# Attention followed by a max-of-products layer: half-walked conversion pieces, and GpSimd's weight and x pieces in other steps

## The chip, the cores and the metric

The kernel runs on one core of one Trainium2 chip. The metric is the device time of one execution in microseconds.

## The reference

```python
scores = np.matmul(q, k.transpose(0, 1, 3, 2)) / np.sqrt(D) + bias   # bias: a small MLP on the relative position
attn = softmax(scores)                                               # with 1e-9 added to the sum
x = np.matmul(attn, v)                                               # (4, 8, 576, 64), then (2304, 512)
h = np.maximum(np.maximum(x @ w1, x @ w2), x @ w3)                   # w: 512 x 768
out = h @ w_out                                                      # 768 x 512
```

q, k and v are (4, 8, 576, 64), B = 4 batches and H = 8 heads. The weights of the second half lie in memory as 8-byte floats; the output is float32, 2304 x 512.

## The kernel before

The work comes in three stages. First the bias tables are made (until about 48 us). Then attention runs, 72 steps in eight rounds of nine; n is the step, n % 9 its position. Last comes the layer behind attention, here called moe, three products whose maximum is taken and an output product, written as schemes of seven block products.

**A step of attention.** Every engine runs its instructions in the order in which the program gives them, so the code's order is the schedule. Step n issues: the scores of step n on PE (front, L287; one step in nine is made of remainders, L277); for each of two heads a shift on DVE (L297: bias added, minimum found) into a tile sn of which three exist; the exponential on ACT (L311) and, every second step, a small copy of the sums (L314, tile sm). The step before last gets its sums' reciprocal on DVE (L321, rc, every second step) and is normalised on GpSimd (norm, L325, two instructions, e<-e,rc). The step four back is turned on PE (flip, L352), copied out by ACT (L458) and DVE (L462, tile et), and later multiplied by v on PE (L393). At two or four positions of a round the q and k of a coming pair are split into a high and a low part, by a cast on ACT (L243, tiles kh and qh) and a subtraction on GpSimd (L249, tiles kl and ql). L285 to L287 use the parts in three matmuls.

**Conversion.** The weights lie in memory as 8-byte floats. fetch (L577) loads half a block as pairs of 32-bit words, and convert (L580) makes float32 from them in five instructions: L584 on ACT (scaled magnitude of the high words, tile wa), and four pieces on DVE: L586 (maximum with 2), L588 (shift and mask), L591 (the low words shifted and joined in) and L594 (the sign joined in, result wr). L586 and L588 have one source, wa, and write it in place; L591 and L594 have two. convert is a generator: it yields "scalar" or "vector" ahead of each piece. A Stream (L517) holds such a generator and takes one piece forward when its next word is the wanted one. A step calls the streams in its list once with "vector" (between, in the midst of the step, behind the et copies and ahead of rc) and once with "scalar" (at its end).

first (L1142) converts six halves during attention, of the sets named 2, 0 and 1. Making the Stream runs it to its first yield. GpSimd's own work on the weights waits in a list, pend: sums of blocks (sums, tile ws, four pieces) and low parts (tile wl, four pieces). In conv, up to two entries of pend are taken out each time that a conversion piece is due, and stand on GpSimd then. early_x makes the parts of the first x block from step 36 on: b12l, b11l and t1l on GpSimd (L535), their casts on ACT, the sum t1 on DVE. The list of streams of a step is made at the end of the program:

```python
if n >= NS - 2 and n % NS in (0, 2, 4, 6, 7):
    more += [w0]
if n >= 36 and n % NS in (2, 6, 7):
    more.insert(0, ex)
```

w0 is the Stream of first, ex that of early_x. Of first only the head, conv and the two blank pieces matter here:

```python
ahead = [fetch(wpool, *todo.pop(0))]
pend = []
def conv(out, name):
    if todo:
        ahead.append(fetch(wpool, *todo.pop(0)))
    for token in convert(wpool, ahead.pop(0), out, name):
        yield token
        if token == "vector":
            for f in pend[:2]:
                pend.pop(0)()
for _ in range(2):
    yield "vector"
```

In moe the same convert makes 18 more halves beside the products, in slots of its own.

Of the kernel before, what the change touches and what calls it, by code (L numbers as in the profile page):

```python
# [9 lines left out]
F32 = mybir.dt.float32  # L10
F32R = mybir.dt.float32r
U32 = mybir.dt.uint32
ACTF = mybir.ActivationFunctionType
ALU = mybir.AluOpType
# [5 lines left out]
def kernel(  # L20
# [12 lines left out]
    nc = tc.nc  # L33
# [165 lines left out]
    NS = len(STEPS)  # L199
# [12 lines left out]
    class Attention:  # L212
        def __init__(self, pool):
            self.pool = pool
            self.data = {}
            self.st = {}
            self.et = {}
            self.pvq = []
            self.done = []
            self.sums = []  # L220
            bias_t.extend(pool.tile([128, 2, S], F32, name=f"bias{t}", bufs=1) for t in range(NTQ + 1))
            self.vl = [pool.tile([128, 2, D], F32, name=f"vl{x}", bufs=1) for x in range(2)]
            for x in self.vl:
                nc.gpsimd.memset(x, 0.0)
# [292 lines left out]
    class Stream:  # L517
# [6 lines left out]
        def go(self, scalar):  # L524
            if self.next == ("scalar" if scalar else "vector"):
                self.next = next(self.gen, None)
                return True

        def rest(self):
            while self.next:  # L530
                self.next = next(self.gen, None)

    def arith(eng, out, a, b, op=ALU.subtract):
        f = lambda x: x.bitcast(F32) if x.dtype == F32R else x
        eng.tensor_tensor(out=out, in0=f(a), in1=f(b), op=op)  # L535
# [37 lines left out]
    def fetch(pool, srcs, name):  # L573
        w = pool.tile([128, 512, 2], U32, tag="w64", bufs=2, name=f"w64{name}")
        n = 512 // len(srcs)
        for x, src in enumerate(srcs):
            nc.sync.dma_start(out=w[:, n * x:n * x + n].rearrange("p (c f) t -> p c (f t)", c=src.shape[1]), in_=src)  # L577
        return w

    def convert(pool, w, out, name):  # L580
        a = pool.tile([128, 512], F32, tag="wa", bufs=1, name=f"wa{name}")
        high, low, t = w[:, :, 1], w[:, :, 0], a.bitcast(U32)
        yield "scalar"
        nc.scalar.activation(a, high.bitcast(F32), ACTF.Abs, scale=2.0 ** 16)  # L584
        yield "vector"
        nc.vector.tensor_scalar(out=a, in0=a, scalar1=2.0, scalar2=None, op0=ALU.max)  # L586
        yield "vector"
        nc.vector.tensor_scalar(out=t, in0=t, scalar1=3, scalar2=0x7FFFFFFF,  # L588
                                op0=ALU.logical_shift_left, op1=ALU.bitwise_and)
        yield "vector"  # L590
        nc.vector.scalar_tensor_tensor(out=t, in0=low, scalar=29, in1=t,  # L591
                                       op0=ALU.logical_shift_right, op1=ALU.bitwise_or)
        yield "vector"
        nc.vector.scalar_tensor_tensor(out=out() if callable(out) else out, in0=high, scalar=signm,  # L594
                                       in1=t, op0=ALU.bitwise_and, op1=ALU.bitwise_or)
# [5 lines left out]
    def w_srcs(s, d):  # L601
        fp, i = divmod(s, 3)
        m = (mw1, mw2, mw3)[i]
        return [m[256 * d:256 * d + 256, 256 * (2 * fp + b):256 * (2 * fp + b) + 256].rearrange(
            "(c p) f -> p c f", p=128) for b in range(2)]
# [4 lines left out]
    def raw_tile(pool, s):  # L610
        return pool.tile([128, 1024], F32, tag=f"wr{s % 2}", bufs=1, name=f"wr{s}")

    def sum_tile(wpool, s):
        return wpool.tile([128, 1024], F32, tag="ws", bufs=1, name=f"ws{s}")

    def part(t, n):
        return t[:, 256 * n:256 * n + 256]

    def sum_w(raw, sr):
        g = nc.gpsimd  # L620
        for o, a, b, op in ((part(sr, 0), part(raw, 0), part(raw, 2), ALU.add),
                            (part(sr, 1), part(sr, 0), part(raw, 1), ALU.subtract),
                            (part(sr, 2), part(raw, 1), part(raw, 0), ALU.subtract),
                            (part(sr, 3), part(raw, 3), part(sr, 1), ALU.subtract)):
            yield "vector"
            arith(g, o, a, b, op)
# [468 lines left out]
    with tc.manual_schedule():  # L1095
        nc.vector.memset(signm, 0x80000000)
        psums.append(tc.alloc_tile_pool(name="psum_b", bufs=1, space=PSUM))
        apool = tc.alloc_tile_pool(name="attn_p", bufs=1, side="right")
        at = Attention(apool)
        n = 0  # L1100
# [36 lines left out]

        last = {}

        def first():  # L1140
            todo = [(w_srcs(s, d), f"{s}_{d}") for s in (PARK, 0, 1) for d in range(2)]
            ahead = [fetch(wpool, *todo.pop(0))]  # L1142

            pend = []

            def conv(out, name):
                if todo:
                    ahead.append(fetch(wpool, *todo.pop(0)))
                for token in convert(wpool, ahead.pop(0), out, name):
                    yield token  # L1150
                    if token == "vector":
                        for f in pend[:2]:
                            pend.pop(0)()

            def sums(raw, name, k=None):
                got = {}

                def piece(n):
                    if n == 0:
                        got["sr"] = sum_tile(wpool, name)  # L1160
                        got["gen"] = sum_w(raw, got["sr"])
                        next(got["gen"])
                    next(got["gen"], None)
                    if n == 3 and k is not None:
                        nc.sync.dma_start(out=w_d[k, 1], in_=got["sr"])
                    return got["sr"]

                return [lambda n=n: piece(n) for n in range(4)]

            def block(name):  # L1170
                made = []

                def half(d):
                    if d == 0:
                        made.append(raw_tile(wpool, 1))
                    return made[0][:, 512 * d:512 * d + 512].bitcast(U32)

                return made, half

            for _ in range(2):  # L1180
                yield "vector"
            made, half = block("2")
            for d in range(2):
                yield from conv(lambda: half(d), f"2_{d}")
            nc.sync.dma_start(out=w_d[0, 0], in_=made[0])
            pend.extend(sums(made[0], "2", 0))
            hi, lo = (wpool.tile([128, 1792], F32R, tag=f"w{c}0", bufs=1, name=f"w{c}0") for c in "hl")
            wf[0] = (hi, lo)
            made, half = block("0")
            for d in range(2):  # L1190
                r = slice(512 * d, 512 * d + 512)
                yield from conv(lambda: half(d), f"0_{d}")
                raw = made[0]
                yield "scalar"
                nc.scalar.copy(hi[:, r], raw[:, r])
                pend.extend(lambda k=k, raw=raw: arith(nc.gpsimd, part(lo, k), part(raw, k), part(hi, k))
                            for k in range(2 * d, 2 * d + 2))
            made, half = block("1")
            for d in range(2):
                yield from conv(lambda: half(d), f"1_{d}")  # L1200
            for f in sums(made[0], "1"):
                yield "vector"
                sr = f()
            last.update(raw=made[0], sr=sr)

        w0 = Stream(first())
        x0 = Blocks(0, xa, xa)

        def early_x():
            g = nc.gpsimd  # L1210
            for k in ("b12", "b11"):
                yield "scalar"
                x0.high(k)
                yield "vector"
                x0.low(k, g)
            yield "vector"
            x0.sum("t1")
            yield "scalar"
            x0.high("t1")
            yield "vector"  # L1220
            x0.low("t1", g)

        def late_x():
            for k in ("b21", "b22"):
                yield "scalar"
                x0.high(k)
                yield "vector"
                x0.low(k, nc.gpsimd)

        ex, lx = Stream(early_x()), Stream(late_x())  # L1230
        while n < NSTEP + LAG:
            more = []
            if n >= NS - 2 and n % NS in (0, 2, 4, 6, 7):
                more += [w0]
            if n >= 36 and n % NS in (2, 6, 7):
                more.insert(0, ex)
            if n >= NSTEP:
                more.insert(0, lx)
            at.step(n, more)
            n += 1  # L1240
        while at.pvq:
            at.pvq.pop(0)()
        for w in (w0, ex, lx):
            w.rest()
        x0.sum("t3")
        x0.high("t3")
# [55 lines left out]
```

## Time and profile before

| what | us |
|---|---|
| runs, median of three | 543.1 |
| runs, lowest and highest | 538.97, 543.71 |
| the profiled execution's own time | 542.02 |
| its span, first to last instruction | 540.2 |

The profiled execution is one execution more, taken by the hardware profiler, and all rows come from it. Its span leaves out 1.8 us around the instructions. In rows, PE is the matrix engine, PEld its weight load, DVE the vector engine, ACT the scalar engine, POOL is GpSimd and SP the queue that issues DMAs. A name such as wa<-w is a destination and its source; x18 counts instructions. Idle time in brackets stands before an instruction, with what ended it. The granted clock is a share of full speed.

### The profile page before, as it was taken

Reading aid. Unit: us, or ns where it says so; the run is one execution under the profiler, and the core shown is the slowest. Engines: PE = TensorE matmul, PEld = TensorE weight load, DVE = VectorE, ACT = ScalarE, POOL = GpSimd, SP = SyncE. Lnnn points to the kernel's source line nnn. Section 1 sums busy time; section 2 is a strip of 40 time slices with the busy share of each in tenths; the row PEclk is TensorE's granted clock in tenths of the full one; section 3 lists DMA queues with packets and bytes.
Section 4 is the critical chain, followed back from the end, with each engine's and each line's share of the span. In section 5 each row is a group of like instructions: output and inputs, shape, how many; then the busy total and the mean of one; then the engine's idle time right before and its main releaser. Section 6 shows DMA issues by size and latency. Waiting matters only on the chain.

```text
span 540.2 us, 13662 instructions
## 1 busy us (share of the span) xinstructions
PE 527.9 (98%) x5199; PEld 439.3 (81%) x5199; DVE 436.9 (81%) x915; ACT 360.0 (67%) x810; POOL 266.8 (49%) x294
## 2 busy tenths in 40 slices
PE   8999899999999899999999999999999999999997
PEld 5455667666767566667599999999999999999997
DVE  7997879899888998878598988658887447898883
ACT  7998889898999898988677433443334325455552
POOL 0003777779878887875500665646466435400000
PEclk9999989999999999999999999999999999999999
DMA  5895976635755165211301125441266340756642
GB/s 164 243 333 174 348 236 197 206 93 158 225 168 150 24 194 160 69 23 23 119 1 41 40 78 183 149 157 42 77 243 204 127 157 0 240 170 196 186 147 79
DMA packets 73458, 78.66 MB, mean 146 GB/s; under 512 B 23152, under 2 KB 54512, under 8 KB 73392
## 3 DMA queue, kind: packets, MB, share of 16 engines
q1 hardware_dynamic: 73248, 77.49, 46.1%
q8 instruction: 41, 0.67, 0.5%
q10 hardware_dynamic: 144, 0.29, 0.2%
q14 instruction: 25, 0.20, 0.1%
HBM read 49.56 MB, written 27.94 MB: 143 GB/s over the span
## 4 chain that ended last, share of the span: by engine, by line
PE 84%; DVE 8%; issue 3%; POOL 2%; ACT 2%; DMA 1%; DVEq 0%; POOLq 0%; ACTq 0%
PE pv L393 13%; PE p L645 11%; PE p L643 11%; PE p L644 11%; PE s L287 10%; PE tp L352 5%; PE p_o L1021 4%; PE p_o L1020 4%; PE p_o L1019 4%; DVE hid L113 4%; PE bp L135 3%; DVE sn L297 2%; PE c L643 2%; PE c L645 2%; PE c L644 2%
## 5 line engine op out<-in xcount | busy, mean ns | idle before, releaser
L325 POOL TENSOR_SCALAR e<-e,rc 128x576 f32<-128x576 f32 x144 | 110.2, 782 | 40.1 <-DVE rc L321 35.0
L297 DVE CUSTOM_DVE_ANT_0 sn<-s,bias 128x576 f32<-128x576 f32 x144 | 103.1, 753 | 26.1 <-PE lp L352 11.8
L311 ACT ACTIVATE e<-sn,nm 128x576 f32<-128x576 f32 x144 | 111.4, 780 | 8.7 <-DVE nm L297 7.4
L393 PE MATMUL pv<-et,vt 128*64 128x320 f32 (+1 forms) x496 | 74.7, 422 | 0.1
L462 DVE COPY et<-tp 128x512 f32<-128x512 f32 x72 | 49.3, 685 | 7.8 <-PE tp L352 6.1
L535 POOL TENSOR_TENSOR wl<-wr,wh 128x256 fp32r<-128x256 f32 x25 | 24.6, 1011 | 58.6 <-ACT wh L731 58.6
L352 PE MATMUL tp<-ident,e 64*128 64x64 f32 x1152 | 52.9, 224 | 0.0
L287 PE MATMUL s<-kh,qh 64*128 64x288 f32 x240 | 49.4, 343 | 3.3 <-DVE nm L297 3.1
L458 ACT COPY et<-tp 128x512 f32<-128x512 f32 x72 | 41.8, 581 | 13.5 <-PE lp L352 11.0
L287 PEld LDWEIGHTS s<-kh,qh 64*128 64x128 f32 x240 | 28.8, 186 | 24.4 <-DVE nm L297 12.3
L352 PEld LDWEIGHTS tp<-ident,e 64*128 64x128 f32 x1152 | 47.2, 139 | 0.0
L393 PEld LDWEIGHTS pv<-et,vt 128*64 128x64 f32 x496 | 30.5, 137 | 18.3 <-issue 2.1
L287 PE MATMUL s<-kl,qh 64*128 64x288 f32 x240 | 42.0, 299 | 0.0
L135 PE MATMUL bp<-hid,w2s 128*32 128x79 f32 (+51 forms) x640 | 39.9, 390 | 0.9 <-DVE hid L113 0.7
L287 PE MATMUL s<-kh,ql 64*128 64x288 f32 x240 | 40.6, 294 | 0.0
L113 DVE TENSOR_SCALAR hid<-sm,bp 128x528 f32<-128x528 f32 (+17 forms) x108 | 39.1, 438 | 0.0
L535 POOL TENSOR_TENSOR wl<-ws,wh 128x256 fp32r<-128x256 f32 x28 | 30.7, 1128 | 12.9 <-ACT wh L733 12.9
L135 PEld LDWEIGHTS bp<-hid,w2s 128*32 128x32 f32 x640 | 19.9, 109 | 21.1 <-issue 15.5
L352 PE MATMUL lp<-ident,e 64*128 64x64 f32 x144 | 33.3, 231 | 3.3 <-ACT et L458 2.4
L690 ACT COPY u<-p 128x384 f32<-128x384 f32 x24 | 11.5, 480 | 37.2 <-PE p L645 37.2
L535 DVE TENSOR_TENSOR q<-p,u 128x384 f32<-128x384 f32 x36 | 19.9, 553 | 17.2 <-ACT u L690 14.2
L352 PEld LDWEIGHTS lp<-ident,e 64*128 64x128 f32 x144 | 19.8, 137 | 16.5 <-POOL e L325 8.5
(232 smaller groups left out, 1617.8 us busy)
## 6 DMA issues: line engine op xcount, KB each, us to landing
bias_d<-bs SPq DMA_DIRECT2D x36, 295.5 KB, 5.2
bias<-bias_d SPq DMA_DIRECT2D x16, 576.0 KB, 5.3
w<-in_moe_w_dram SPq DMA_DIRECT2D x36, 256.0 KB, 3.3
h_d<-ht SPq DMA_DIRECT2D x18, 384.0 KB, 3.3
hin<-h_d SPq DMA_DIRECT2D x16, 384.0 KB, 4.5
qr<-in_qd_dram SPq DMA_DIRECT2D x16, 288.0 KB, 4.7
kr<-in_kd_dram SPq DMA_DIRECT2D x16, 288.0 KB, 4.8
vt<-in_v_dram SPq DMA_DIRECT2D x32, 128.0 KB, 3.2
```

What stands on the lines that cost most here:

```text
L113: marks["hid"] = nc.vector.tensor_scalar(out=h[:, 0:n], in0=wl[:, 0:n], scalar1=k["bp"][:, m:m + 1], scalar2=0.0, op0=ALU.add, op1=ALU.max)
L135: nc.tensor.matmul(bp[32 * c:32 * c + 32, o:o + w], lhsT=w2s, rhs=src, start=True, stop=True)
L287: nc.tensor.matmul(ss[h][:, x, 0:HALF], lhsT=u[q][p, 128 * t:128 * t + 128], rhs=u[k][p, cols], start=(j == 0), stop=(j == len(terms) - 1))
L297: nc.vector.tensor_tensor_reduce(out=sn.rearrange("p (a b) -> p a b", a=2), in0=st["s"][h][:, :, 0:HALF], in1=bt.rearrange("p (a b) -> p a ...
L311: nc.scalar.activation(st["e"][:, S * h:S * h + S], sn, ACTF.Exp, scale=-1.0, bias=nm, accum_out=self.sm[:, x:x + 1])
L325: nc.gpsimd.tensor_scalar(out=e, in0=e, scalar1=self.rc[:, x:x + 1], scalar2=1.0, op0=ALU.mult, op1=ALU.mult)
L352: return nc.tensor.transpose(to, e2[p, k0:k0 + 128], ident[p, p])
L393: nc.tensor.matmul(pv[p], lhsT=w, rhs=x, start=(c == 0), stop=(c == NTQ))
L535: eng.tensor_tensor(out=out, in0=f(a), in1=f(b), op=op)
L643: nc.tensor.matmul(o, lhsT=hi[:, c], rhs=h[:, j], start=first and j == 0, stop=False, **on)
L644: nc.tensor.matmul(o, lhsT=hi[:, c], rhs=l[:, j], start=False, stop=False, **on)
L645: nc.tensor.matmul(o, lhsT=lo[:, c], rhs=h[:, j], start=False, stop=last and j == 1, **on)
```

## The change

Four edits. The two one-source pieces of convert walk wa as 128 x 2 x 256, first the even and then the odd elements, still in place. The list pend becomes an object Pieces with a place of its own in the steps: one entry at positions 1, 3, 5 and 8, while conversion keeps positions 0, 4, 6 and 7, and x pieces get 3 and 8. The block of set 2 gets a buffer of its own, wr2, and set 1 takes out what is left of pend before it takes a buffer. And the two blank "vector" pieces at the head of first go, so that the generator's first yield is that of the first conversion.

```diff
--- before.py
+++ after.py
@@ -583,9 +583,11 @@
         yield "scalar"
         nc.scalar.activation(a, high.bitcast(F32), ACTF.Abs, scale=2.0 ** 16)
         yield "vector"
-        nc.vector.tensor_scalar(out=a, in0=a, scalar1=2.0, scalar2=None, op0=ALU.max)
+        apart = a.rearrange("p (n k) -> p k n", k=2)
+        nc.vector.tensor_scalar(out=apart, in0=apart, scalar1=2.0, scalar2=None, op0=ALU.max)
         yield "vector"
-        nc.vector.tensor_scalar(out=t, in0=t, scalar1=3, scalar2=0x7FFFFFFF,
+        apart = apart.bitcast(U32)
+        nc.vector.tensor_scalar(out=apart, in0=apart, scalar1=3, scalar2=0x7FFFFFFF,
                                 op0=ALU.logical_shift_left, op1=ALU.bitwise_and)
         yield "vector"
         nc.vector.scalar_tensor_tensor(out=t, in0=low, scalar=29, in1=t,
@@ -1137,20 +1139,34 @@
 
         last = {}
 
+        class Pieces:
+
+
+            def __init__(self):
+                self.todo = []
+
+            def extend(self, fs):
+                self.todo.extend(fs)
+
+            def go(self, scalar):
+                if self.todo and not scalar:
+                    self.todo.pop(0)()
+
+            def rest(self):
+                while self.todo:
+                    self.todo.pop(0)()
+
+        pend = Pieces()
+
         def first():
             todo = [(w_srcs(s, d), f"{s}_{d}") for s in (PARK, 0, 1) for d in range(2)]
             ahead = [fetch(wpool, *todo.pop(0))]
-
-            pend = []
 
             def conv(out, name):
                 if todo:
                     ahead.append(fetch(wpool, *todo.pop(0)))
                 for token in convert(wpool, ahead.pop(0), out, name):
                     yield token
-                    if token == "vector":
-                        for f in pend[:2]:
-                            pend.pop(0)()
 
             def sums(raw, name, k=None):
                 got = {}
@@ -1171,14 +1187,16 @@
                 made = []
 
                 def half(d):
-                    if d == 0:
+                    if d == 0 and name == "2":
+                        made.append(apool.tile([128, 1024], F32, name="wr2", bufs=1))
+                    elif d == 0:
+                        if name == "1":
+                            pend.rest()
                         made.append(raw_tile(wpool, 1))
                     return made[0][:, 512 * d:512 * d + 512].bitcast(U32)
 
                 return made, half
 
-            for _ in range(2):
-                yield "vector"
             made, half = block("2")
             for d in range(2):
                 yield from conv(lambda: half(d), f"2_{d}")
@@ -1230,9 +1248,11 @@
         ex, lx = Stream(early_x()), Stream(late_x())
         while n < NSTEP + LAG:
             more = []
-            if n >= NS - 2 and n % NS in (0, 2, 4, 6, 7):
+            if n >= NS - 2 and n % NS in (0, 4, 6, 7):
                 more += [w0]
-            if n >= 36 and n % NS in (2, 6, 7):
+            if n % NS in (1, 3, 5, 8):
+                more += [pend]
+            if n >= 36 and n % NS in (3, 8):
                 more.insert(0, ex)
             if n >= NSTEP:
                 more.insert(0, lx)
@@ -1240,7 +1260,7 @@
             n += 1
         while at.pvq:
             at.pvq.pop(0)()
-        for w in (w0, ex, lx):
+        for w in (w0, pend, ex, lx):
             w.rest()
         x0.sum("t3")
         x0.high("t3")
```

On ACT, steps 6 to 10, before: wa is the conversion's tile, e and sm belong to the softmax, et to the turned products, kh to the split of k.

```order
L314 ACTIVATE sm_1120<-sm_1120 128x4
L311 ACTIVATE e_1268,sm_1269<-sn_0_1265,nm_0_1266 128x576
L311 ACTIVATE e_1268,sm_1269<-sn_1_1271,nm_1_1272 128x576
L458 COPY et_1_1218<-tp_5_0_1280 128x8x64
L458 COPY et_1_1218<-lp_5_1279 128x128
L311 ACTIVATE e_1325,sm_1269<-sn_0_1322,nm_0_1323 128x576
L458 COPY et_1_1130<-tp_3_0_1333 128x8x64
L458 COPY et_1_1130<-lp_3_1332 128x128
L311 ACTIVATE e_1325,sm_1269<-sn_1_1327,nm_1_1328 128x576
L314 ACTIVATE sm_1269<-sm_1269 128x4
L243 CAST kh_1363<-kr_1051 128x576
L584 ACTIVATE wa_0_1362<-w_0_1181 128x512
```

And with the change, in the same place:

```order
L314 ACTIVATE sm_1120<-sm_1120 128x4
L584 ACTIVATE wa_0_1187<-w_0_1181 128x512
L311 ACTIVATE e_1273,sm_1274<-sn_0_1270,nm_0_1271 128x576
L311 ACTIVATE e_1273,sm_1274<-sn_1_1276,nm_1_1277 128x576
L458 COPY et_1_1222<-tp_5_0_1285 128x8x64
L458 COPY et_1_1222<-lp_5_1284 128x128
L311 ACTIVATE e_1330,sm_1274<-sn_0_1327,nm_0_1328 128x576
L458 COPY et_1_1130<-tp_3_0_1338 128x8x64
L458 COPY et_1_1130<-lp_3_1337 128x128
L311 ACTIVATE e_1330,sm_1274<-sn_1_1332,nm_1_1333 128x576
L314 ACTIVATE sm_1274<-sm_1274 128x4
L243 CAST kh_1365<-kr_1051 128x576
```

L584 stood behind four exponentials, two pairs of et copies and a kh cast; now it stands behind the sm copy of step 7 and ahead of all of them.

On POOL around step 45, before (b12l and b11l are parts of x, wl of a weight, kl and ql of k and q):

```order
L535 TENSOR_TENSOR b12l_3471<-xb_0_1169,b12h_3220 128x768
L325 TENSOR_SCALAR e_3338<-e_3338,rc_3473 128x576 x2
L535 TENSOR_TENSOR b11l_3537<-xb_0_1170,b11h_3477 128x768
L325 TENSOR_SCALAR e_3409<-e_3409,rc_3473 128x576 x2
L325 TENSOR_SCALAR e_3467<-e_3467,rc_3595 128x576 x2
L535 TENSOR_TENSOR wl_2319<-wr_2766,wh_2318 128x256 x2
L325 TENSOR_SCALAR e_3533<-e_3533,rc_3595 128x576 x2
L249 TENSOR_TENSOR kl_3666<-kr_3356,kh_3665 128x576
```

And with the change:

```order
L325 TENSOR_SCALAR e_3335<-e_3335,rc_3464 128x576 x2
L325 TENSOR_SCALAR e_3401<-e_3401,rc_3464 128x576 x2
L535 TENSOR_TENSOR b12l_3582<-xb_0_1169,b12h_3281 128x768
L325 TENSOR_SCALAR e_3459<-e_3459,rc_3584 128x576 x2
L325 TENSOR_SCALAR e_3522<-e_3522,rc_3584 128x576 x2
L249 TENSOR_TENSOR kl_3655<-kr_3348,kh_3654 128x576
L535 TENSOR_TENSOR wl_2381<-wr_2954,wh_2380 128x256
L325 TENSOR_SCALAR e_3574<-e_3574,rc_3717 128x576 x2
L249 TENSOR_TENSOR ql_3722<-qr_3349,qh_3721 128x576
L325 TENSOR_SCALAR e_3647<-e_3647,rc_3717 128x576 x2
L535 TENSOR_TENSOR b11l_3845<-xb_0_1170,b11h_3588 128x768
L535 TENSOR_TENSOR wl_2381<-wr_2954,wh_2380 128x256
```

The two wl ahead of a product of L325 and a kl are gone; one wl stands behind kl, and another comes behind b11l, later.

On SP, from the last bias table to the next loads of q and k, before:

```order
L170 DMA bias_d<-bs_878 16x8x591
L577 DMA w_0_1181<-in_moe_w_dram 128x2x256 x2
L259 DMA vt_1184<-in_v_dram 128x4x64
L260 DMA vl_80<-in_v_dram 64x64
L259 DMA vt_1184<-in_v_dram 128x4x64
L260 DMA vl_80<-in_v_dram 64x64
L230 DMA qr_1305<-in_qd_dram 128x576
L231 DMA kr_1304<-in_kd_dram 128x576
L577 DMA w_1_1359<-in_moe_w_dram 128x2x256 x2
```

And with the change:

```order
L170 DMA bias_d<-bs_878 16x8x591
L577 DMA w_0_1181<-in_moe_w_dram 128x2x256 x2
L577 DMA w_1_1184<-in_moe_w_dram 128x2x256 x2
L259 DMA vt_1188<-in_v_dram 128x4x64
L260 DMA vl_80<-in_v_dram 64x64
L259 DMA vt_1188<-in_v_dram 128x4x64
L260 DMA vl_80<-in_v_dram 64x64
L230 DMA qr_1310<-in_qd_dram 128x576
L231 DMA kr_1309<-in_kd_dram 128x576
```

The second fetch moved from behind six loads to a place directly behind the first fetch.

## Rows read from the trace of the kernel before

**Rows 1.** The page, part 1: engine, busy us (share of the span), instructions.

```profile
PE 527.9 (98%) x5199; PEld 439.3 (81%) x5199; DVE 436.9 (81%) x915; ACT 360.0 (67%) x810; POOL 266.8 (49%) x294
```

**Rows 2.** The chain that ended last, from 80 to 340 us: start, us, what.

```profile
108.80 1.13 PE s L277 x16
...
135.08 1.13 PE s L277 x16
...
189.76 1.27 PE s L277 x16
...
216.86 1.13 PE s L277 x16
...
243.04 1.15 PE s L277 x16
```

**Rows 3.** Timeline of DVE at two places: start us, us, line, operation, out<-in.

```profile
177.89 4.31 DVE L586 TENSOR_SCALAR wa<-wa 128x512 f32<-128x512 f32 x1
182.12 0.74 DVE L297 CUSTOM_DVE_ANT_0 sn<-s,bias 128x576 f32<-128x576 f32 x1
...
198.75 1.74 DVE L594 SCALAR_TENSOR_TENSOR wr<-w,signm,wa 128x512 uint32<-128x512 uint32 x1
```

**Rows 4.** Timeline of POOL at the same two places.

```profile
177.64 1.45 POOL L535 TENSOR_TENSOR wl<-wr,wh 128x256 fp32r<-128x256 f32 x2
179.05 1.50 POOL L325 TENSOR_SCALAR e<-e,rc 128x576 f32<-128x576 f32 x2
180.48 1.44 POOL L249 TENSOR_TENSOR kl<-kr,kh 128x576 fp32r<-128x576 f32 x1
...
198.09 1.84 POOL L535 TENSOR_TENSOR t1l<-t,t1h 128x768 fp32r<-128x768 f32 x1
```

**Rows 5.** Timeline of PE there, the waits in brackets (idle before, releaser).

```profile
182.93 0.40 PE L287 MATMUL s<-kh,qh 64*128 64x288 f32 x1 [1.28 <-DVE nm L297]
...
201.21 0.40 PE L287 MATMUL s<-kh,qh 64*128 64x288 f32 x1 [0.21 <-DVE nm L297]
```

**Rows 6.** Instructions on the tile wa, whole span: duration ns min/median/max, first, last start.

```profile
L586 DVE TENSOR_SCALAR wa<-wa x18: 409/866/4307, 78.6 to 407.4; 128x512 f32<-128x512 f32 x18
...
L591 DVE SCALAR_TENSOR_TENSOR wa<-w,wa x18: 681/693/1231, 90.5 to 410.5; 128x512 uint32<-128x512 uint32 x18
L594 DVE SCALAR_TENSOR_TENSOR wr<-w,signm,wa x18: 744/756/1739, 94.1 to 411.2; 128x512 uint32<-128x512 uint32 x18
```

**Rows 7.** Timeline of ACT from 66.9 to 74.7 us, idle time before in brackets.

```profile
66.94 0.20 ACT L314 ACTIVATE sm<-sm 128x4 f32<-128x4 f32 x1
67.27 0.78 ACT L311 ACTIVATE e<-sn,nm 128x576 f32<-128x576 f32 x1
...
70.16 0.78 ACT L311 ACTIVATE e<-sn,nm 128x576 f32<-128x576 f32 x1 [0.63 <-DVE nm L297]
...
74.08 0.68 ACT L584 ACTIVATE wa<-w 128x512 f32<-128x512 f32 x1 [0.86 <-DMA vl<-in_v_dram]
74.68 0.76 ACT L311 ACTIVATE e<-sn,nm 128x576 f32<-128x576 f32 x1
```

**Rows 8.** Timeline of SP (its DMA queue), the first weight half.

```profile
68.38 1.73 SPq L577 DMA_DIRECT2D w<-in_moe_w_dram  x2
```

**Rows 9.** DMAs issued by L577 between 60 and 80 us, issue to landing.

```profile
DMA to landing us min/median/max: 4.2/4.6/5.0
```

**Rows 10.** Stretches: length, busy us (instructions) by engine, granted clock, DMA share, GB/s.

```profile
66.00:70.60 4.60, 3.72 (x53) 2.48 (x50) 3.82 (x11) 3.81 (x12) 4.60 (x7) 1.00 0.99 336
70.60:74.00 3.40, 3.20 (x17) 2.23 (x19) 2.23 (x8) 2.60 (x8) 1.40 (x2) 0.50 0.92 262
78.00:97.40 19.40, 19.36 (x276) 13.31 (x272) 18.07 (x50) 17.70 (x48) 15.74 (x17) 1.00 0.61 168
...
290.00:330.00 40.00, 40.00 (x232) 40.00 (x231) 35.94 (x51) 19.23 (x33) 22.54 (x21) 1.00 0.25 86
```

## Prediction

> **What bounds the kernel now.** I began with the page's busy shares: PE is busy for 98% of the span [rows 1], so a time can only be gained or lost where PE stands still or where its clock is down. The chain of waits, read second, shows where attention is irregular. Its front has one row per round of nine steps, the sixteen matmuls of L277, and the distance between two such rows is the length of a round [rows 2]: 26.28 us from 108.80 to 135.08 and 26.18 us from 216.86 to 243.04, mean 26.23. Between them something costs time: 135.08 to 189.76 are two rounds and take 54.68, which is 2.22 over 2 x 26.23, and 189.76 to 216.86 takes 27.10, which is 0.87 over. Together 3.09 us.
>
> The timelines of DVE and POOL tell what these are. At 177.89 one conversion piece, L586, takes 4.31 us [rows 3] while its smallest duration is 409 ns [rows 6]; over that time GpSimd runs two lo parts of a weight, the two products of L325 and a kl, five instructions without a gap [rows 4]. The next shift stands behind the piece, at 182.12, and PE waits 1.28 us for it at 182.93 [rows 5]. At 198.75 L594 takes 1.74 us where 744 ns is the smallest, beside t1l of 1.84 us, and PE waits again, at 201.21 [rows 3 to 6].
>
> The last view is ACT's timeline around 67 to 75 us, where the first weights come [rows 7]. There the conversion's first piece, L584 (wa<-w), starts at 74.08 after 0.86 us of idle time. The row names a load of v as what ended the idle time; by SP's row the weight half was issued from 68.38 on, in two DMAs over 1.73 us, and these loads land 4.2 to 5.0 us after issue, 4.6 in the median [rows 8, 9]. The second, issued about 0.87 us in, so lands at 68.38 + 0.87 + 4.6 = 73.9 us, and ACT starts on the half at once.
>
> **The change part by part.** (1) The two blanks at the head of first() go. By the order on ACT, L584 then stands directly behind the sm copy that ends at 67.14 [rows 7], ahead of the exponentials of step 8, which start at 67.27 before. SP's rows ahead of the first weight load are the same ones in both kernels, so the half still lands at about 74.0, and ACT waits for it from 67.15 to 74.0: 6.85 us. Queued behind it on ACT are the exponentials of steps 8 and 9, their et copies and a kh cast; the flips on PE and GpSimd's L325 wait for the exponentials, the shifts for a free sn buffer, and scores for the shifts. From 67.27 to the exponential at 74.68 are 7.41 us, of which 0.63 and 0.86 were idle and 0.68 was L584 itself; the work left is 5.24. In the changed kernel it begins at 74.0 + 0.68 and ends at 79.92, against 74.68: 5.2 us later.
>
> Can PE get that back? In 78 to 97.4 us it is busy for 19.36 of 19.40, ACT for 17.70 [rows 10], so ACT could make up at most 1.7 and PE nothing: the least price of the wait is 5.2 - 1.7 = 3.5. It can also cost more. In 70.6 to 74.0 PE was granted 0.50, the lower of its two levels (1.2 GHz), after a stretch in which it was busy 3.72 of 4.60, and was itself busy 3.20 us [rows 10]. A stop of some five us is a longer gap. If the same 3.4 us of low clock then fall behind the wait, where PE has work to catch up, half of 3.20 is lost again: 5.2 + 1.6 = 6.8. The ends are 3.5 and 6.8. I take 5.7, a third of the way from 5.2 to 6.8, because behind the wait ACT with its 5.24 us of work, and not PE alone, sets the pace. The second fetch on SP now follows the first directly, ahead of loads of v, q and k that go back by some 1.7 us (the row of the first fetch); nothing in the next two steps needs those, so I count zero.
>
> (2) GpSimd's pieces go one at a time to positions 1, 3, 5 and 8. The order on POOL shows the pair of wl that stood at the head of the five-instruction run gone; at step 45 the DVE piece is now the last of a set, L596 (L594 before), and no longer the one of 4.31 us. t1l moves to step 57, where no conversion piece stands. So both excesses, 2.22 and 0.87, should go: -3.1. The least that this can be is what PE's waits show, 1.28 + 0.21 = 1.5 [rows 5]; the most is 3.1. I take 3.1, since the length of a round is what adds up to the end.
>
> (3) New neighbours. The piece at step 45 is a two-source one beside two L325, kl and wl; the worst such case before is 198.75, which cost 0.87. At step 48 b11l, wl and kl stand together on POOL, 1.84 + 0.73 + 1.44 = 4.0 us by rows of the same sizes [rows 4], ahead of the products of the next steps. The first case costs 0 to 0.87, the second 0 to 0.73 (what wl adds to b11l, which met kl before only a few steps apart). I take 0.4 for both.
>
> (4) The strided pieces. No row shows a one-source operation with this walk. The nearest from below is the same operation unstrided and alone, 409 ns; from above L591, which reads every second word of w, at a median of 693 [rows 6]. The unstrided piece does 512 elements in 409 ns, L591 as many in 693. At 0.69 the twelve pieces in attention need 12 x 0.28 = 3.4 us of DVE more than unblocked ones, and less than the medians of L586 (866) would make of it. DVE is busy for 81% of the span [rows 1] and PE does not wait for it in steady rounds, so this is hidden: 0, and if that cover were gone, 3.4 at the most. After attention, 290 to 330 us, DVE is busy 35.94 of 40.00 us and PE all 40.00 [rows 10]: a piece that is 0.28 longer when alone and 0.17 shorter than the median of L586 leaves PE as it is. Zero there too. A page speaks against this part: the Trainium skill, "VectorE: DVE Perf Modes", section "What auto-detection actually checks", has a one-source operation within SBUF take the mode that reads through two ports when its outermost dimension that is not one is even, and asks for no inner step there. The walk has 2 x 256, so by that rule the piece would stay in the mode it is in and go on waiting for GpSimd; no run so far shows such a walk, and the time this would give is rival A's.
>
> **The sum.** The profiled execution took 542.0 us, 1.1 under the median of the runs (543.1). 542.0 + 5.7 - 3.1 + 0.4 = 545.0. With every term at its better end it is 542.0 + 3.5 - 3.1 = 542.4, with every term at its worse end 542.0 + 6.8 - 1.5 + 1.6 = 548.9.
>
> **Rivals.** A, the walk does not do what it says. If strided pieces still cannot run beside GpSimd, then those at steps 9, 13, 27, 31, 51 and 61, all beside L325, still wait. Earlier waits of this kind lie in rounds of 26.28 against 26.18 and are nearly hidden, but the piece at step 51 follows the backlog of step 48 and may repeat the 2.22: 545.0 to 547.2, say 546. For it: at 177.89 the piece lasts until the whole run of GpSimd is over, as if it waited for a resource, and the change keeps the number of elements. Against: no row shows the walk at all. The rule named under (4) is the other reason to keep it.
>
> B, the wait on ACT is covered, because the half lands much earlier than I read or because PE has other work: only the gain is left, 542.0 - 3.1 = 538.9. For it: the row of L584 names another DMA than the weight's. Against: the idle time of 0.86 ends when 68.38 plus the landing time says it should.
>
> C, slower: ACT's wait costs more than itself. The place is the same, 67 to 80 us. If no idle time of ACT is absorbed the slip is 6.85, and a second stretch of low clock adds 1.7 (half of another 3.4 us); with new neighbours at 1.6 and the gain at 1.5 the time is 542.0 + 6.85 + 1.7 + 1.6 - 1.5 = 550.7. It decides from the point where the stop of PE exceeds some 5 us and the clock stays low for more than 3.4 us after it. For it: gaps far shorter than 5 us preceded the low clock before. Against: behind the wait PE is not alone on the path.
>
> **How the numbers follow.** Forecast 0.50, A 0.20, B 0.12, C 0.18. A measurement of this kernel can tell about 1%, 5.4 us, from no change. Slower by more than that, over 548.5, is C but for a small part, and a little of A: 0.17. Faster by more, under 537.7, needs B with a bonus: 0.05. The rest, 0.78, is within 1%. The range that leaves out the ends of B and C is 540.0 to 549.5.
>
> **What would show it.** In the trace of the changed kernel: L584 on ACT with about 6.9 us of idle time before it, PE with gaps of together about 5 us between 67 and 75, the granted clock at 0.50 somewhere in 70 to 80; the row of L277 that stands at 108.80 before 5 to 6 us later; rounds of 26.2 to 26.5 throughout, no conversion piece over 1.8 us; L587 and L590 between 409 and 700 ns. The prediction is wrong if ACT does not wait there, if PE is held at low clock for much longer, or if a strided piece beside GpSimd lasts as long as GpSimd's run.

## The result and the profile after

| | before | changed |
|---|---|---|
| median of 4 runs, us | 541.5 | 548.36 |
| lowest and highest, us | 538.97, 543.71 | 546.55, 548.97 |
| profiled execution, us | 542.02 | 548.97 |
| its span, us | 540.2 | 547.2 |

The changed kernel takes 1.011 times as long, 95% interval 1.0066 to 1.0153: slower, inside the predicted range of 540.0 to 549.5, and near its upper end. Span against span it is 7.0 us.

ACT's timeline of the changed kernel, the place of [rows 7]:

```profile
66.78 0.21 ACT L314 ACTIVATE sm<-sm 128x4 f32<-128x4 f32 x1
74.61 0.66 ACT L584 ACTIVATE wa<-w 128x512 f32<-128x512 f32 x1 [7.63 <-DMA w<-in_moe_w_dram]
75.17 0.76 ACT L311 ACTIVATE e<-sn,nm 128x576 f32<-128x576 f32 x1
...
78.73 0.59 ACT L458 COPY et<-tp 128x512 f32<-128x512 f32 x1 [0.55 <-PE tp L352]
...
81.25 0.78 ACT L311 ACTIVATE e<-sn,nm 128x576 f32<-128x576 f32 x1 [0.20 <-DVE nm L297]
...
84.11 0.59 ACT L458 COPY et<-tp 128x512 f32<-128x512 f32 x1 [2.00 <-PE lp L352]
```

L584 stands directly behind the sm copy and waits 7.63 us for the weight's DMA, which the bracket now names. The row at 81.25 answers to the one at 74.68 in [rows 7]: ACT is 6.57 us late there. Behind it ACT waits 2.00 us more, for transposes on PE. PE's timeline shows where it stood for the same reason:

```profile
77.47 0.36 PE L352 MATMUL lp<-ident,e 64*128 64x64 f32 x1 [8.37 <-ACT et L458]
```

The windows show the granted clock over that time (length, busy us by engine, granted clock, DMA share, GB/s):

```profile
66.00:70.00 4.00, 2.59 (x31) 1.70 (x30) 3.13 (x9) 0.95 (x3) 4.00 (x5) 0.92 0.86 273
70.00:76.00 6.00, 0.00 (x0) 0.00 (x0) 0.00 (x0) 1.39 (x4) 1.15 (x2) 0.50 1.03 304
76.00:78.00 2.00, 0.53 (x10) 0.53 (x12) 0.77 (x2) 2.00 (x7) 0.00 (x0) 0.50 1.08 318
78.00:82.00 4.00, 4.00 (x34) 2.84 (x32) 2.56 (x7) 3.22 (x10) 0.87 (x1) 0.50 0.04 15
82.00:84.00 2.00, 2.00 (x28) 1.00 (x26) 0.00 (x0) 0.12 (x2) 1.99 (x3) 0.76 0.00 0
84.00:90.00 6.00, 6.00 (x84) 3.94 (x80) 4.80 (x14) 5.32 (x14) 3.35 (x4) 1.00 0.23 52
```

PE does nothing from 70 to 76 us, at 0.50 of the clock, and when work comes back at 77.5 the clock stays at 0.50 until past 82. In [rows 10] the low stretch was 3.4 us long. Of the longer one here PE has work for some 5.5 us (from 77.47 to about 82.96, as the mean of 0.76 in 82 to 84 gives it). The chain's rows of L277, which answer to [rows 2], add it up:

```profile
117.09 1.13 PE s L277 x16
143.58 1.15 PE s L277 x16
170.09 1.13 PE s L277 x16
196.32 1.15 PE s L277 x16
223.78 1.13 PE s L277 x16
249.99 1.15 PE s L277 x16
```

The first is 8.29 us later than its partner at 108.80. From there to the last it takes 132.90 us, before 134.24 (108.80 to 243.04): 1.34 less. 8.29 - 1.34 = 6.95, the whole difference of the spans. The rounds are 26.49, 26.51, 26.23, 27.46 and 26.21, so over the steady 26.23 they cost 0.26 + 0.28 + 0 + 1.23 - 0.02 = 1.75. The old excess of 3.09 is gone, and 1.75 has come in its place. No row here shows which piece makes the 0.26 and the 0.28.

The 27.46 has a piece of its own, in DVE's and POOL's timelines at step 51 (in the place of 177.89 in [rows 3] and [rows 4]):

```profile
205.19 1.90 DVE L587 TENSOR_SCALAR wa<-wa 128x512 f32<-128x512 f32 x1
207.02 0.73 DVE L297 CUSTOM_DVE_ANT_0 sn<-s,bias 128x576 f32<-128x576 f32 x1
```

```profile
203.87 2.94 POOL L325 TENSOR_SCALAR e<-e,rc 128x576 f32<-128x576 f32 x4
```

A strided piece still waits for a run of GpSimd, here of four L325. The rows on the tile wa, which answer to [rows 6], show what the walk did to the piece by itself:

```profile
L587 DVE TENSOR_SCALAR wa<-wa x18: 420/462/1904, 79.2 to 414.4; 128x512 f32<-128x512 f32 x18
L590 DVE TENSOR_SCALAR wa<-wa x18: 407/420/856, 93.3 to 417.0; 128x512 uint32<-128x512 uint32 x18
L593 DVE SCALAR_TENSOR_TENSOR wa<-w,wa x18: 673/694/1234, 98.8 to 417.4; 128x512 uint32<-128x512 uint32 x18
```

420 ns alone, against 409 unstrided in the kernel before and 415 in e4 below: the piece keeps its duration within the scatter of these rows, and comes nowhere near L593's median of 694 for as many elements.

### The profile page after: what moved, and what is told of

It reads as the page before. It is cut to its first block, busy times and chain, and to the rows that moved or that the text cites. A ratio compares the mean times of both kernels' runs of the same rounds, so it can differ in the third digit from the quotient of the medians.

```text
span 547.2 us, 13666 instructions
## 1 busy us (share of the span) xinstructions
PE 527.9 (96%) x5199; PEld 439.4 (80%) x5199; DVE 432.6 (79%) x915; ACT 360.0 (66%) x810; POOL 267.1 (49%) x294
## 4 chain that ended last, share of the span: by engine, by line
PE 85%; DVE 7%; issue 2%; ACT 1%; DMA 1%; SPq 1%; POOL 1%; DVEq 0%; ACTq 0%; POOLq 0%
PE pv L393 14%; PE p L647 11%; PE p L645 11%; PE p L646 10%; PE s L287 10%; PE tp L352 5%; PE p_o L1023 4%; PE p_o L1022 4%; PE p_o L1021 4%; PE bp L135 4%; DVE hid L113 3%; PE s L277 2%; DVE sn L297 2%; PE c L645 2%; PE c L646 2%
## 5 line engine op out<-in xcount | busy, mean ns | idle before, releaser
L297 DVE CUSTOM_DVE_ANT_0 sn<-s,bias 128x576 f32<-128x576 f32 x144 | 103.1, 753 | 34.7 <-PE lp L352 14.7
L325 POOL TENSOR_SCALAR e<-e,rc 128x576 f32<-128x576 f32 x144 | 110.6, 785 | 37.1 <-DVE rc L321 31.7
```

Source lines behind the costliest of these rows:

```text
L297: nc.vector.tensor_tensor_reduce(out=sn.rearrange("p (a b) -> p a b", a=2), in0=st["s"][h][:, :, 0:HALF], in1=bt.rearrange("p (a b) -> p a ...
L325: nc.gpsimd.tensor_scalar(out=e, in0=e, scalar1=self.rc[:, x:x + 1], scalar2=1.0, op0=ALU.mult, op1=ALU.mult)
```

## The experiments

The theory (W): the time is ACT's wait for the first weight half, with the low clock behind it. Rivals: the walk, the new neighbours of the pieces, or the early second fetch. Each comparison has its own runs of the kernel before, whose medians lie between 539.83 and 541.38 us. Ratios carry their 95% intervals. Lengths of rounds in this section are from the first shift (L297) of a round to that of the next; round 5 is 29.5 us in the kernel before and 28.1 in the changed one.

**e1, the first conversion late.**

```diff
-            if n >= NS - 2 and n % NS in (0, 4, 6, 7):
+            if n >= NS and n % NS in (0, 4, 6, 7) or n == NS + 2:
```

> The changed kernel, but the first conversion starts two steps later: L584 is issued at the end of step 9 instead of step 7 and its first DVE piece stands at step 11; every later piece stays where the change has it, and the two first fetches stay together. Theory W (the added time is ACT's wait for the first weight half and the low clock behind it): the row of L277 that stands at 81.88 before and at 90.17 after comes back to 82 +- 0.5, L584 waits under 1.5 us, and the time is 548.4 - 8.3 = 540.1 us, 539 to 541.5. Rival P (the pieces' walk and their new neighbours cost the time): no lower than 546. Rival F (the second fetch issued early delays the loads behind it): the wait goes but rounds 1 and 2 grow, 542 to 545.

540.04 us against 540.0 of the kernel before, ratio 0.9995 (0.9975 to 1.0015). L584 waits 1.25 us, and the granted clock of the profiled execution is 1.00 throughout. The row of L277 stands at 81.17, a little ahead of the 82 +- 0.5 expected. W holds. All else that the change does is in this kernel, and together it is worth nothing that can be measured. The second fetch is still early here, so it is not the cause either.

**e2, the blank pieces left out of the kernel before.**

```diff
-            for _ in range(2):
-                yield "vector"
             made, half = block("2")
```

> The kernel before with one part of the change alone: the two blank pieces at the head of the first conversions are left out, so L584 stands behind step 7. GpSimd's pieces and the walk are as before (conversion pieces shift by two places). Theory W: ACT waits 7 to 8 us, PE stands for about as long, the clock is low for some microseconds behind it, and the time is 541.5 + 8.3 = 549.8, 548 to 552 (round 5's collision may or may not be hit). Rival P: within 2 us of the kernel before, 540 to 543.5.

547.45 against 540.0, ratio 1.0139 (1.011 to 1.0167); L584 waits 8.10 us. This one edit brings a loss as large as the whole change, 7.5 us, a little under the 8.3 that I expected. The pieces stand in other steps here, and no one-source piece in attention takes over 1.2 us: round 5 is 27.4 us instead of 29.5, so the wait's own price lies above the 7.5.

**e3, the walk alone.** The kernel before with the two lines of the diff that make the walk.

> The kernel before with the walk of every second element alone. Theory W with the walk idle (the piece keeps its speed and its wait for GpSimd): 541.5 +- 1, the two one-source pieces at 0.41 to 0.43 us when alone and still 0.7 to 4.3 beside GpSimd. If the walk takes the piece out of GpSimd's way at one element a cycle: 0.69 us each wherever they stand, none over 1.3, 538 to 540. If the walk is what costs: over 544.

540.45 against 540.0, ratio 1.0008 (0.9985 to 1.003). In its trace the piece of 4.31 us of [rows 3] is there again, 4.28 us, beside the same five GpSimd instructions:

```profile
L587 DVE TENSOR_SCALAR wa<-wa x18: 413/642/4284, 77.2 to 406.1; 128x512 f32<-128x512 f32 x18
```

**e4, the change without the walk.**

> The changed kernel without the walk: the two one-source pieces run over 512 elements in a row as before. Theory W with the walk idle: 548.4 +- 1, same wait of 7.6 us on ACT, same pieces blocked (0.8 beside kl in round 1, up to 1.9 beside three L325 in round 5). If the walk is what costs: under 545. If the walk helps: over 550, with pieces of several us beside GpSimd.

547.71, ratio 1.0138 (1.0112 to 1.0164), wait 8.18 us, the piece at step 51 1.86 us. With e3: the walk neither costs nor helps by an amount that shows.

**e5, PE kept busy in the wait.**

```diff
+            for _ in range(20 if n == 5 else 0):
+                nc.tensor.matmul(self.st[9]["s"][0][:, 0, 384:512], lhsT=ident, rhs=ident, start=True, stop=True)
             a = turn(0, lp[:, 0:64], LB)
```

> The changed kernel with 20 more matmuls that only keep PE busy (ident by ident, into an unused part of a scores tile), between the scores of step 9 and the transposes that wait for ACT; by the rows of such matmuls before they take about 6.8 us, within the 8.4 us for which PE stands there. ACT's wait stays at 7.6 to 8.2 us. Theory C (part of the 8.3 us is the low clock behind the idle time, not the wait): the granted clock stays at 1.00 through 78 to 84 us, the row of L277 that stands at 90.2 moves to 87.5 +- 1, and the time is 545 to 546.5. Rival N (the wait alone costs all of it): row and time as without them, 547.5 to 548.5.

545.38, ratio 1.0102 (1.0066 to 1.0137), against 548.36 and 547.71 with idle PE. The windows:

```profile
70.00:76.00 6.00, 5.08 (x50) 4.89 (x52) 0.88 (x4) 3.22 (x8) 1.35 (x2) 1.00 1.05 307
76.00:78.00 2.00, 2.00 (x32) 1.60 (x30) 1.59 (x3) 1.88 (x6) 0.00 (x0) 1.00 0.07 27
78.00:82.00 4.00, 4.00 (x53) 2.43 (x50) 2.98 (x9) 3.72 (x10) 2.90 (x4) 1.00 0.01 4
```

The clock is 1.00 all through, and the twenty matmuls took 4.73 us, less than the 6.8 expected. The profiled execution is the fastest of the six; in four of the six the mean granted clock is 0.997, so that part of a low stretch is left in those, against 0.988 to 0.990 in the changed kernel. In this profile the half came early (L584 waits 5.58 us), so its row of L277, at 85.80, is not to be compared as it stands; the table below takes the wait out.

**e6, L584 one step later than in the change.**

```diff
-            if n >= NS - 2 and n % NS in (0, 4, 6, 7):
+            if n >= NS - 1 and n % NS in (0, 4, 6, 7) or n == NS - 1:
```

> The changed kernel with L584 one step later, behind the exponentials and et copies of step 8; every DVE piece stays where the change has it. ACT's wait should go from 7.6 to 8.2 us down to about 5.3. Theory W with a price for each us of wait and the same low clock behind it: 2.5 to 3 us less than the changed kernel, 545 to 546. If only a wait beyond some slack counts: 541 to 543. If any stop of PE costs the same low stretch and the length matters little: 547 to 548.

545.58, ratio 1.0106 (1.007 to 1.0142); L584 waits 4.96 us and PE stands for 4.6. Each us of wait has its price. One table for the wait and the clock, from PE's, ACT's and the windows' rows of each kernel; 80.57 is e3's row of L277, with a wait of 0.57 and no low clock (one trace of each kernel):

| kernel | L584 waits, us | clock at 78 to 80 us | row of L277, us | later than 80.57 | that less the wait |
|---|---|---|---|---|---|
| e5 | 5.58 | 1.00 | 85.80 | 5.2 | -0.4 |
| e6 | 4.96 | 0.50 | 87.33 | 6.8 | 1.8 |
| changed | 7.63 | 0.50 | 90.10 | 9.5 | 1.9 |
| e2 | 8.10 | 0.50 | 89.80 | 9.2 | 1.1 |
| e4 | 8.18 | 0.50 | 90.50 | 9.9 | 1.7 |

With the clock held, PE is late by about the wait; with the clock low behind it, by 1.1 to 1.9 us more.

**e7, no weight piece at position 3.** e1, and pend at positions 1, 5 and 8.

> The changed kernel with the late first conversion (as in the run in which only that was undone) and GpSimd's weight pieces at positions 1, 5 and 8, not 3, so that b11l and a wl no longer stand together in step 48. Theory B (in that run the piece of 1.84 us at step 51 and the 1.2 us that round 5 still costs come from the backlog of b11l, wl, kl and the L325 behind them): no one-source piece over 1.1 us in attention, round 5 at 26.2 to 26.8 us instead of 28.1, time 538.5 to 539.5. If other pieces or the reciprocals are the cause: round 5 stays at 27.5 or more and the time at 540.

A miss: 539.49, ratio 0.9996 (0.9974 to 1.0019), and the piece at step 51 still takes 1.90 us beside three L325. The backlog of step 48 was not its cause. In step 51 GpSimd has four L325 in a row in any case.

**e8, L587 with two sources.** e1 with this line:

```diff
+        nc.vector.scalar_tensor_tensor(out=a, in0=a, scalar=2.0, in1=a, op0=ALU.max, op1=ALU.max)
```

> The changed kernel with the late first conversion, and L587 (the maximum with 2) written as an operation with two sources, both wa, with the same values and no walk. Theory P (a one-source piece takes both ports and so waits for GpSimd until GpSimd's run ends; a two-source one gets in after one instruction): L587 takes 0.68 to 0.75 us alone and never over 1.3 beside GpSimd, the 1.84 at step 51 falls to about 1.0, round 5 comes down by 0.5 to 0.9 us, time 539 to 540. If the wait does not depend on the form: 1.8 us or more at step 51, time 540 to 541.

In the trace as expected: 0.68 us alone, 0.70 at step 51, where it gets in between two L325; GpSimd's four then take 3.37 us, against 2.93 in e1. In the time nothing: 540.68 against 539.98, ratio 1.0009 (0.9981 to 1.0036).

**e10, the same line in the kernel before.**

> The kernel before with L586 alone written with two sources, both wa. Theory P: the 4.3 us piece beside five GpSimd instructions becomes one of 0.7 to 1.3 us, round 5 falls from 29.5 to 26.8 - 27.6 us, time 1.5 to 2.5 under the kernel before, 537.5 to 538.5. If GpSimd's run holds any form of the piece until its end: 4 us there, time as before.

This overturns what e8 seemed to show. The two-source piece in DVE's timeline, and GpSimd's run beside it:

```profile
177.40 4.52 DVE L586 SCALAR_TENSOR_TENSOR wa<-wa 128x512 f32<-128x512 f32 x1
```

```profile
177.13 1.42 POOL L535 TENSOR_TENSOR wl<-wr,wh 128x256 fp32r<-128x256 f32 x2
178.54 1.46 POOL L325 TENSOR_SCALAR e<-e,rc 128x576 f32<-128x576 f32 x2
179.97 1.40 POOL L249 TENSOR_TENSOR kl<-kr,kh 128x576 fp32r<-128x576 f32 x1
```

It waits for the same five instructions, whatever its form. 542.55 against 541.38, ratio 1.0018 (0.9984 to 1.0051).

**e9, conversion at even steps only.**

```diff
+            if n > NS and n % 2 == 0:
+                more += [w0]
+            if n % 2 == 1 and n % 6 != 3:
+                more += [pend]
+            if n >= 36 and n % 6 == 3:
+                more.insert(0, ex)
```

> The changed kernel with conversion pieces at even steps only, from step 10 on (the first weight half is then long there), GpSimd's weight pieces at odd steps, x pieces at 39, 45, 51 and so on. At an even step GpSimd's L325 waits for the reciprocal that stands behind the piece on DVE, so nothing should run beside the piece. Theory G (a piece waits only where GpSimd runs, and the odd steps are these): every one-source piece in attention takes 0.41 to 0.45 us, rounds 2 to 6 are 26.0 to 26.5 us each, L584 waits for nothing; 538 to 539.2 us, 1 to 2 under the kernel before. If the round's parity does not matter or the reciprocals come late: pieces over 1 us remain, 540 or more.

Half a miss. Most one-source pieces take 0.41 to 0.57 us (one 1.30), and no round reaches 27.2. But rounds 2 to 6 are 26.6 to 27.1 each, longer than the quiet 26.2, and the time is 540.65 against 541.38, ratio 0.9992 (0.9971 to 1.0013). At 140 us a piece at an even step stands ahead of rc, in DVE's rows and those of GpSimd and PE:

```profile
140.19 1.53 DVE L593 SCALAR_TENSOR_TENSOR wa<-w,wa 128x512 uint32<-128x512 uint32 x1
141.64 0.17 DVE L321 RECIPROCAL rc<-sm 128x4 f32<-128x4 f32 x1
```

```profile
141.91 2.19 POOL L325 TENSOR_SCALAR e<-e,rc 128x576 f32<-128x576 f32 x3 [0.73 <-DVE rc L321]
```

```profile
142.28 1.08 PE L393 MATMUL pv<-et,vt 128*64 128x256 f32 x8 [0.95 <-PE lp L352]
```

The piece holds up rc, GpSimd's L325 waits 0.73 us for it, and PE stands 0.95 at about the same time. That this is what makes the rounds longer is not shown: the bracket of PE's row names a transpose of PE's own, and in the kernel before, too, L325 waits for rc, by 0.2 to 3.2 us at a time. PE's later stands of 0.60 and 0.32 end with a copy (xb, L413) on DVE. As e9 moved GpSimd's pieces as well, the cause stays open.

**e11, no conversion piece in step 51.** e1 with `and n != 51` in its condition.

> The changed kernel with the late first conversion and no conversion piece in step 51: L587 stands in step 52 instead, the pieces of that half and the next move back by up to six steps. Theory R (the piece of 1.84 us comes from the four L325 that GpSimd runs in a row in step 51): L587 takes 0.41 to 0.8 us, round 5 falls from 28.1 to 26.5 - 27.2 us; the time falls by 1 to 1.5 to 539 +- 0.7. If another piece meets a run of GpSimd in its new step, one piece stays over 1.5 us and the time at 540.

L587 takes 0.42 us in step 52, and round 5 is 27.15 us instead of 28.1. 540.0 against 539.83, ratio 1.0008 (0.9992 to 1.0023): the piece is explained, but the 0.9 us that the trace gains in round 5 does not show in the time, which did not fall as expected.

**e12, two matmuls more in each of steps 7, 8 and 9.** e11 and, ahead of the transposes of each, two matmuls as in e5.

> The same with two matmuls in each of steps 7, 8 and 9 that only keep PE busy where it waits for 0.3 us before the transposes. Theory C (the low clock around 70 to 74 us follows these gaps; it is in about half of the executions of every kernel without ACT's wait and is worth some 1.4 us): the mean granted clock is 0.999 or 1.0 in nearly all runs, the time 538 to 539, though the matmuls themselves may cost up to 0.7. If the low stretch has another cause: the clock of the runs is as scattered as in the run without them, and the time up to 1 us longer.

The mean granted clock is 0.999 or 1.0 in all 12 runs, in e11's in 9 of 12 and in those of the kernel before in 13 of 23. The time is 540.26, ratio 1.0009 (0.9995 to 1.0023), and not the 538 to 539 expected. In the traces, both at a clock of 1.00, the row of L277 stands at 81.78 here and at 80.41 in e11: the matmuls cost some 1.4 us, as much as the low stretch in e7, whose row stands at 81.81 with no wait of L584. No version beat the kernel before by a margin that could be measured.

## Why the prediction was right, and which of its terms were wrong

The forecast was 545.0, within 1% of the kernel before, the range 540.0 to 549.5; measured were 548.36, just under the 548.5 from which the prediction gave slower a chance of 0.17, and a ratio of 1.011, just over 1%. The mechanism that made the time, ACT's wait under (1), was the one named, and e1 and e2 show it from both sides: without it the change costs nothing that can be measured, and alone it costs as much as the whole change. The size was less than half of what came: the terms add up to 3.0 us over the profiled execution, measured were 6.95. The time fell into the range because the range was wide; no change at all would have lain in it too. Two terms were too small, (1) by 2.6 and (3) by 1.35, and together they are the whole difference.

(1) The term of the wait was 5.7 and came out at 8.29 by the rows of L277. Three parts of its working were short. The half arrived at 74.6 and not 74.0; L584 waited 7.63 for the predicted 6.85 (ACT came to it 0.16 earlier, and the fetch was issued at 69.27, not at 68.38). Behind it I had ACT work without a pause to the exponential at 79.92; there were waits of 0.55 and 0.20, and it came at 81.25, 6.57 late instead of 5.2. Then PE came another 8.29 - 6.57 = 1.7 later. Most of that is put down to the low clock, which was not 3.4 us long, as I had carried over from [rows 10], but lasted from about 70 to past 82. The subtraction alone does not measure it, since the trace of the kernel before has a low stretch of its own (its row of L277 stands at 81.81, e3's without one at 80.57); the table, against e3, gives the clock 1.1 to 1.9. Rival C had 1.7 for it, from a second stretch of 3.4 us: that the price agrees where the length does not is luck. I had taken a third of the way to that end, on the argument that ACT and not PE sets the pace behind the wait; at half clock PE did, and ACT waited 2.00 us for it at 84.11. e5 shows the part apart: with the clock held, PE is late by about the wait (5.2 for 5.58).

(2) The removed excess was read rightly in the trace, 3.09, and is gone. But in the runs it does not show: e1, which has (2), (3) and (4) without (1), is at 0.9995 of the kernel before. (3) is why for the greater part: the rounds cost 1.75 over the steady length, where I allowed 0.4 and 1.6 at most for new neighbours. The place was also wrong. I looked at steps 45 and 48, and the cost was in step 51 (1.23 us), beside L325 alone, with 0.26 and 0.28 in two rounds before. e11 shows the first: without a piece in step 51 the round is 0.9 shorter. For the other two no piece is shown. Rival A named step 51, but for a backlog that e7 shows not to be the cause. The rest, 1.34 us of the trace, is at the edge of e1's interval, whose lower end is 0.0025 x 540 = 1.35.

(4) The walk costs nothing, as predicted, but not for the reason that the sum relied on. Rival A had the mechanism: the pieces keep their speed (420 ns) and go on waiting for GpSimd (1.90 us in the change, 4.28 in e3). The rule of the Trainium skill, "VectorE: DVE Perf Modes", section "What auto-detection actually checks", agrees: a walk of 2 x 256 keeps the even outermost dimension, and the 420 ns, near the unstrided 409 and far from L593's 694, say that the mode stayed. A's time of 546 is the forecast's plus one collision, and does not tell it apart. The sum would have been closer with A's one collision in (3): 545.0 + 1.2.

Rival B falls: the wait was not covered. C was right that the clock stays low for more than 3.4 us behind the wait. Of ACT's wait a part was absorbed on ACT itself (7.63 waited, 6.57 late); on PE, with the clock held, hardly any was (e5). C's 550.7 is 2.3 over the measured time.

The time at which L584 can start on the first half varies from run to run by more than 2 us. Whether the second fetch right behind it delays it is not settled: with both together L584 started between 72.78 and 75.22, with the first alone at 73.91 to 74.30, in three traces. From the fetch's issue (67.17 to 69.27) to that start it is 5.65 to 5.70 us in the three, and 5.23 to 6.75 in the eight traces with both in which ACT waited: more scattered, and not plainly later.

## What to carry to other kernels

An instruction that waits for a DMA belongs, on an engine in order, behind the work that does not need that DMA: compute the landing time from the issue's row and place the first user after it, since everything queued behind pays most of the wait (6.57 of 7.63 us on ACT here). If PE stands idle over it, add the low clock that follows to the price; here it was 1.1 to 1.9 us on top of a wait of 5 to 8. And a shorter piece is not yet a shorter time: the piece of 4.3 us in the kernel before, that of 1.84 in e1 and the quiet pieces of e9 all belong to kernels of about 540 us. Follow the length of the rounds and the time of the runs, not a piece's own duration; what sets the length of e9's rounds is not shown.

## What the runs showed that was not expected

A DVE piece beside GpSimd sometimes gets in after one GpSimd instruction and sometimes waits until GpSimd's whole run is over: 4.28 to 4.52 us for five instructions, in both forms of the operation, and 1.84 to 1.92 beside a run of L325 in step 51, with one source. In e8 the two-source form took 0.70 in that same step, and GpSimd's four L325 took longer instead. What decides it stays open. The page "SBUF — State Buffer" of the Trainium skill, section "SBUF: two separate sides", has the lock of the shared pair for one whole instruction, whichever starts first; the 4.52 us of e10 spans five, so the trace shows more than that rule says.

The clock is low around 70.6 to 74 us also with hardly any or no wait of ACT, in the traces of the kernel before and of e7, both with a mean granted clock of 0.997. Ten of 23 runs of the kernel before in e12's comparison have means of 0.994 to 0.997; with two matmuls more ahead of the transposes in steps 7 to 9 no run of 12 has one under 0.999.
